# Moving the weights to another DMA queue and re-ranking a planner's tasks in an fp32 threshold-attention and feed-forward kernel

## The chip, the cores and the metric

The kernel runs on one core of a Trainium2 chip. Its metric is the device time of one execution in microseconds (us); lower is better. All times quoted are medians of several executions in the fast state. The span, which the profile uses, runs from the first to the last instruction of one profiled execution and lies 1.7 to 2.2 us under that execution's time. Engines are named as in the profile: PE is TensorE, DVE is VectorE, ACT is ScalarE, POOL is GpSimd, SP is SyncE. A name with a small q behind it ("SPq") is that engine's sequencer issuing DMAs.

## The reference

Attention in which all scores lower than the row's maximum minus tau are dropped, then a feed-forward layer with a sigmoid-weighted activation, all in fp32:

```python
# q, k, v: (8, 8, 576, 64); tau = 0.02; w_in: (512, 2048); w_out: (2048, 512)
scores = scale * np.matmul(q, k.transpose(0, 1, 3, 2))
thresh = np.max(scores, axis=-1, keepdims=True) - tau
scores = np.where(scores >= thresh, scores, -1000000000.0)
scores = scores - np.max(scores, axis=-1, keepdims=True)
attn = np.exp(scores)
attn = attn / (np.sum(attn, axis=-1, keepdims=True) + 1e-09)
x = np.matmul(attn, v)            # then (8, 8, 576, 64) -> (4608, 512)
h = x @ w_in
g = h * (1.0 / (1.0 + np.exp(-1.702 * h)))
out = g @ w_out
```

The two weights arrive as 64-bit floats (they are scaled by 1/np.sqrt of an integer), so the kernel converts 32 pieces of 128 x 512 elements to fp32 itself.

## The kernel before

Two heads make a pair; there are 32 pairs. For each pair the kernel loads q, k and v, transposes q and k on VectorE, multiplies them on TensorE, copies the scores to SBUF on ScalarE, finds each query's maximum on VectorE, subtracts it there, masks and exponentiates on ScalarE, and multiplies with v on TensorE. When the four pairs of a batch item are done, blocks of 512 tokens go through the feed-forward layer, which is most of TensorE's work.

Nothing of the order is left to a compiler. Each piece of work is a `task` with an engine, an estimated cost, a rank, and buffers that it takes and gives back. A small planner simulates the engines and, whenever one is free, emits the ready task of the lowest rank. The rank of a pair's tasks is its number, so the emitted order of each engine follows from ranks and costs; at run time each engine works through its list in order. The early pairs borrow space that the feed-forward layer uses later, so a tile of theirs can be named gT; early weight pieces likewise pass through w_out.

```python
def task(engine, cost, rank, f, *a, after=(), take=(), give=(), lag=0.06):
    tasks.append((engine, cost, rank, f, a, [x for x in after if x is not None],
                  take, give, lag))
    return len(tasks) - 1
...
def load_qk(n, which, queue):              # one of a pair's q or k: 4 transfers
    ...
    for h in range(2):
        for j in range(2):
            queue.dma_start(               # rows of 32 fp32 = 128 bytes
                out=blocks[ds(64 * h + 32 * j, 32), :, :],
                in_=src[b, 2 * hp + h, :, ts(j, 32)].rearrange("(c p) d -> p c d", p=32),
            )
...
def load_w(i):                             # one weight piece, 64-bit: rows of 4 KB
    ...
    nc.sync.dma_start(out=t.rearrange("p c w -> p (c w)"), in_=dram.bitcast(U32))
    nc.sync.dma_start(                     # the same bytes again, shifted by 3
        out=t3.rearrange("p c w -> p (c w)").bitcast(U8)[:, 0 : 8 * WC - 3],
        in_=dram.bitcast(U8)[:, 3 : 8 * WC],
    )
...
def sub(n, t):                             # score * scale - (maximum * scale - tau)
    ...
    nc.vector.scalar_tensor_tensor(
        out=s, in0=s, scalar=scl, in1=mb, op0=ALU.mult, op1=ALU.subtract
    )
...
def exps(n, t):
    nc.scalar.activation(out=s, in_=s, func=AF.Exp, bias=shift)
...
# ranks: weights, and all the tasks of pair n
rank = NPAIR - 0.4 + 0.5 * i / n_in if i < n_in else NPAIR - 0.16 + 0.9 * (i / n_in - 1)
...
r = float(n)                               # loads of q and k: r - 2.0; of v: r - 1.2
```

Two transfers per weight piece, 32 pieces and 512 KB each make 33.5 MB. SyncE issues nearly all transfers of the kernel (ScalarE issues only pair 0's k), so a weight piece stands in one line with q, k and v.

Of the kernel before, what the change touches and what calls it, by code (L numbers as in the profile page):

```python
# [19 lines left out]
P = 128  # L20
GELU_SCALE = 1.702
EPS = 1e-9

# [6 lines left out]
def kernel(  # L30
# [33 lines left out]
    NKT = 4  # L64
# [14 lines left out]
    work = ctx.enter_context(tc.tile_pool(name="work", bufs=2))  # L79
    psA = ctx.enter_context(tc.tile_pool(name="psA", bufs=3, space=bass.MemoryType.PSUM))  # L80
# [6 lines left out]
    kd = [const.tile([P, P], FP32, name=f"kd{i}") for i in range(2)]  # L87
# [4 lines left out]
    tau_b = const.tile([P, 1], FP32, name="tau_b")  # L92
    scl = const.tile([P, 1], FP32, name="scl")
    shift = const.tile([P, 1], FP32, name="shift")
# [6 lines left out]
    limits = {"psA": 3, "psM": 2, "s_m": 7, "s_t": 2, "io": 3, "xT": 3, "mb": 1,  # L101
              "raw0": 1, "raw1": 1, "qkT0": 1, "qkT1": 1, "v_m": 2, "w64": 2}
# [3 lines left out]

    def task(engine, cost, rank, f, *a, after=(), take=(), give=(), lag=0.06):
        tasks.append((engine, cost, rank, f, a, [x for x in after if x is not None],
                      take, give, lag))
        return len(tasks) - 1  # L110

# [117 lines left out]
    def load_w(i):  # L229
        dst, src, c, j = pieces[i]  # L230
        dram = src[ts(c, P), ts(j, WC)]
        if not wide:
            nc.sync.dma_start(out=dst[:, c, ts(j, WC)], in_=dram)
            return


        x = stage(i)
        if x is None:
            t = work.tile([P, WC, 2], U32, name="w64", tag="w64", bufs=2)
            t3 = work.tile([P, WC, 2], U32, name="w64s", tag="w64s", bufs=2)  # L240
        else:
            rows = [w_out[:, ds(PER_STAGE * x + 2 * y, 2), :] for y in range(2)]
            t, t3 = (
                r.rearrange("p a b -> p (a b)").bitcast(U32).rearrange("p (c w) -> p c w", w=2)
                for r in rows
            )
        nc.sync.dma_start(out=t.rearrange("p c w -> p (c w)"), in_=dram.bitcast(U32))
        nc.sync.dma_start(
            out=t3.rearrange("p c w -> p (c w)").bitcast(U8)[:, 0 : 8 * WC - 3],
            in_=dram.bitcast(U8)[:, 3 : 8 * WC],  # L250
        )
        cv[i] = t[:, :, 1], t[:, :, 0], t3[:, :, 0]
# [37 lines left out]
    mats, sT, stats, mbs, pss = {}, {}, {}, {}, {}  # L290
# [7 lines left out]
    def prep_kd(n):  # L298
        for h in range(2):
            nc.scalar.copy(  # L300
                out=kd[n % 2][ts(h, D), ts(h, D)], in_=mats[n, 1][ts(h, D), MAIN:S]
            )
# [4 lines left out]
    def scores(n, t, c):  # L307
        qT, kT = mats[n, 0], mats[n, 1]
        ps = psA.tile([P, 2, 512], FP32, name="ps", tag="ps")
        if t == NKT:  # L310
            for i in range(2):
                nc.tensor.matmul(  # L312
                    ps[:, i, 0:SH], lhsT=kd[n % 2], rhs=qT[:, ts(i, SH)],
                    start=True, stop=True,
                )
            del mats[n, 0], mats[n, 1]
        else:
            for h in range(2):
                nc.tensor.matmul(  # L319
                    ps[:, h, 0:SH],  # L320
                    lhsT=kT[ts(h, D), ts(t, P)], rhs=qT[ts(h, D), ts(c, SH)],
                    start=True, stop=True,
                )
        pss[n, t, c] = ps

    def keep(n, t, c):
# [3 lines left out]
        else:  # L330
            if c == 0:
                st = home(n, "s_m", 2 * S, "s_m", 7, f"s_m{t}")
# [7 lines left out]
    def in_groups(n, t, op):  # L340

        if (n, op) not in stats:
            stats[n, op] = [
                work.tile([P, NKT, 2 * QB], FP32, name="part", tag="part", bufs=2),
                work.tile([P, QB], FP32, name="part_t", tag="part_t", bufs=3),
# [8 lines left out]
    def over_tiles(n, op):  # L354

        pm, pt = stats[n, op]
        r = work.tile([P, 2 * QB], FP32, name="red", tag="red", bufs=3)
# [8 lines left out]
    def over_groups(n, op):  # L366
        r = stats[n, op]
        o = work.tile([64, 2 * QB], FP32, name="fold", tag="fold")
# [4 lines left out]
    def lower(n):  # L373
# [3 lines left out]
            out=f[0:32], in0=stats[n, ALU.max][0:32], scalar1=scl[0:32],  # L377
            scalar2=tau_b[0:32], op0=ALU.mult, op1=ALU.subtract,
# [3 lines left out]
        stats[n, ALU.max] = f  # L382

# [6 lines left out]

    def sub(n, t):
        mb, s = mbs[n], sT[n, t]
        if t < NKT:
            nc.vector.scalar_tensor_tensor(  # L394
                out=s, in0=s, scalar=scl, in1=mb, op0=ALU.mult, op1=ALU.subtract
            )
        else:
            for h in range(2):
                x = s[ts(h, D)]
                nc.vector.scalar_tensor_tensor(  # L400
                    out=x, in0=x, scalar=scl[ts(h, D)], in1=mb[ts(h, D), h, :],
                    op0=ALU.mult, op1=ALU.subtract,
                )
# [5 lines left out]
    def exps(n, t):  # L409
        s = sT[n, t]  # L410
        nc.scalar.activation(out=s, in_=s, func=AF.Exp, bias=shift)  # L411
# [58 lines left out]
    def spread_sums(n):  # L470
# [3 lines left out]
        rc = work.tile([P, S], FP32, name="rc", tag="rc")  # L474
# [63 lines left out]
    nc.sync.dma_start(  # L538
        out=tau_b, in_=bass.AP(tensor=tau.tensor, offset=tau.offset, ap=[[0, P], [1, 1]])
    )  # L540
    for t in kd + v_t + [ones_t]:
        nc.gpsimd.memset(t, 0.0)
    nc.gpsimd.memset(ones, 1.0)
    nc.gpsimd.memset(rebias, -896.0 * 2.0**23)
    for h in range(2):
        nc.gpsimd.memset(ones_t[ts(h, D), h, :], 1.0)

    def tau_terms():



        nc.vector.tensor_scalar(
            out=scl, in0=tau_b, scalar1=0.0, scalar2=SCALE, op0=ALU.is_ge, op1=ALU.mult
# [4 lines left out]
        nc.vector.tensor_single_scalar(out=shift, in_=tau_b, scalar=-1.0, op=ALU.mult)  # L558




    FIRST, LAST = -1.0, 1000.0
    BY_PE = 5
    LEAD = 6

    ready_w = []
    for i in range(len(pieces)):
        rank = NPAIR - 0.4 + 0.5 * i / n_in if i < n_in else NPAIR - 0.16 + 0.9 * (i / n_in - 1)
        if not wide:  # L570
            ready_w.append(task("SP", 0.6, rank, load_w, i, lag=2.5))
# [3 lines left out]
        a = task("SP", 1.1, rank, load_w, i, take=place, lag=5.0)  # L575
        e = task("DVE", 0.44, rank, cv_ex, i, after=[a])
        m = task("ACT", 0.72, rank, cv_power, i, after=[e])
# [3 lines left out]
        ready_w.append(task("DVE", 0.72, rank, cv_end, i, after=[a, m] + over, give=place))  # L581

    tau_done = task("DVE", 1.0, -2.0, tau_terms)
# [5 lines left out]
    def feed_forward(blk):  # L589
        b = -(-(blk + 1) * BLK // S) - 1  # L590
        xs = [placed[n] for n in range(NPAIR * (b + 1))]
        for j in range(NFC):
            for p in range(2):
                after = ffn[-1:] + xs[-NPAIR:]
                if blk == 0:
# [3 lines left out]
                    "PE", 1.79, LAST, mm1, blk, j, p, after=after,  # L599
# [4 lines left out]
                "DVE", 0.7, FIRST, gelu, j, after=[a, last_mm2.get(j // 2)],  # L604
                give=("psM", "io"),
            )
        for i in range(BLK // P):
            for p in range(NFC // 2):
                after = ffn[-1:] + [gelus[2 * p], gelus[2 * p + 1]]
                if blk == 0:  # L610
# [3 lines left out]
                    "PE", 1.79, LAST, mm2, i, p, after=after, take=("psM",) if p == 0 else (),  # L614
# [10 lines left out]
    for n in range(NP):  # L625
        gate = per_pair * (n - LEAD)
        after = ffn[gate : gate + 1] if gate >= 0 else []
        r = float(n)
        q0, q1 = (nc.sync, nc.scalar) if n == 0 else (nc.sync, nc.sync)
# [3 lines left out]
        pq = task("DVE", 0.78, r, prep, n, 0, after=[lq], take=own(n, "qkT0"), give=own(n, "raw0"))  # L633
        pk = task("DVE", 0.78, r, prep, n, 1, after=[lk], take=own(n, "qkT1"), give=own(n, "raw1"))
        pd = task("ACT", 0.5, r, prep_kd, n, after=[pk])
        mx = []
        for t in range(NKT + 1):
            tail = t == NKT
            copies = []
            for c in range(1 if tail else 2):  # L640

                a = task(
                    "PE", 1.1 if tail else 0.58, r, scores, n, t, c,
                    after=[pq, pk] + ([pd] if tail else []) + after,
                    take=("psA", "s_t") if tail else ("psA",) + (own(n, "s_m") if c == 0 else ()),
                    give=own(n, "qkT0", "qkT1") if tail else (),
                )
                after = [a]
                copies.append(task("ACT", 0.64, r, keep, n, t, c, after=[a], give=("psA",)))
            mx.append(task("DVE", 0.78 if tail else 1.37, r, in_groups, n, t, ALU.max, after=copies))  # L650
        a = task("DVE", 0.75, r, over_tiles, n, ALU.max, after=mx)
        a = task("DVE", 0.75, r, over_groups, n, ALU.max, after=[a])
        a = task("DVE", 0.6, r, lower, n, after=[a, tau_done])
        m = task("DVE", 1.38, r, spread_max, n, after=[a], take=own(n, "mb"))
        ws, subs = [], [m]
        for t in range(NKT + 1):
            tail = t == NKT
            a = task(
                "DVE", 1.5 if tail else 1.37, r, sub, n, t, after=subs[-1:],
                give=own(n, "mb") if tail else (),  # L660
            )
            subs.append(a)
            a = task("ACT", 0.7 if tail else 1.17, r, mask, n, t, after=[a])
            ws.append(task("ACT", 0.88 if tail else 1.36, r, exps, n, t, after=[a]))
        back = own(n, "s_m") * NKT + ("s_t",)
        every = range(NKT + 1)
        if n < NPAIR:

            pv = den = None
            for t in every:  # L670
                first = t == 0
                den = task(
                    "PE", 1.1, r, sums_by_pe, n, [t], True, after=[ws[t], den],
# [3 lines left out]
                    "PE", 1.1, r, values, n, [t], after=[ws[t], den, pv, lv],  # L677
                    take=("psA",) if first else (), give=(back[t],) if t < NKT else ("s_t", "v_m"),
                )
            a = task("DVE", 1.2, r, one_row, n, after=[den], give=("psM", "psM"))  # L680
        else:
            pv = task("PE", 5.0, r, values, n, every, after=ws + [lv], take=("psA",), give=("v_m",))
        if NPAIR <= n < BY_PE:
            a = task("PE", 5.2, r, sums_by_pe, n, every, False, after=ws + [pv], take=("psA",), give=back)
            a = task("DVE", 1.2, r, one_row, n, after=[a], give=("psA",))
        elif n >= BY_PE:
            su = [
                task("DVE", 0.78 if t == NKT else 1.37, r, in_groups, n, t, ALU.add, after=[ws[t]])
                for t in range(NKT + 1)
            ]  # L690
            a = task("DVE", 0.75, r, over_tiles, n, ALU.add, after=su + [pv], give=back)
            a = task("DVE", 0.75, r, over_groups, n, ALU.add, after=[a])
            a = task("DVE", 0.7, r, one_group, n, after=[a])
        a = task("DVE", 1.05, r, spread_sums, n, after=[a])
        b, hp = divmod(n, NPAIR)
        new = {(b * S + x) // BLK for x in cuts(b)[:-1]} if hp == 0 else set()
        if b:
            new -= {(b * S - 1) // BLK}
        placed[n] = task(
            "DVE", 0.9, r, place_x, n, after=[a, pv], take=("xT",) * len(new), give=("psA",)  # L700
# [35 lines left out]
```

## Time and profile before

| | before |
|---|---|
| time, median of 4 | 1448.2 us (1447.3 to 1449.3) |
| span | 1446.5 us |
| TensorE busy / idle | 1384.0 / 62.5 us |
| first matmul | 7.95 us |
| pair 5's last subtraction ends | 219.2 us |
| pair 5's values start on TensorE | 226.66 us |

Three more views matter for what follows. The first is SyncE's queue in the timeline before: start, duration, line, what is loaded. The first two lines are the issues of pair 1's q and k (the early pairs borrow space that the feed-forward layer uses later, so the tile is named gT; early weight pieces likewise pass through w_out):

```profile
6.64 2.20 SPq L189 DMA_DIRECT2D gT<-in_q_dram  x4
8.89 2.12 SPq L189 DMA_DIRECT2D gT<-in_k_dram  x4
...
29.12 5.58 SPq L189 DMA_DIRECT2D gT<-in_q_dram  x4
34.80 4.99 SPq L189 DMA_DIRECT2D gT<-in_k_dram  x4
```

Four issues take 2.1 to 2.2 us. The duration is that of the issuing, not of the transfer: the page gives a median of 2.3 us from issue to landing for each single one of q_raw's transfers. The last two lines are pair 3's q and k, which stand directly behind the first weights in the same queue: there the issuing takes 5.58 and 4.99 us, but VectorE does not wait for them. The second view is the busy time of each engine in two stretches, before and after 40 us, up to 330 us, from where TensorE is full (from 330 to 1420 us it is busy for 1089.95 to 1090.00 of 1090 us in the six kernels of this study that were asked for it):

```profile
0.00:40.00 40.00, 22.32 (x132) 13.14 (x132) 28.91 (x47) 22.13 (x32) 1.34 (x13) 0.87 0.84 228
40.00:330.00 290.00, 248.94 (x1037) 119.26 (x1035) 260.20 (x434) 164.02 (x219) 0.00 (x0) 0.92 0.40 120
```

The columns are the stretch, its length, then busy us (and instructions) of PE, PE's weight loads, DVE, ACT and POOL, then the granted clock, the DMA engines' share and GB/s. VectorE's third pair of numbers is the one to follow: 28.9 us of work in the first 40, and 289.1 us in the first 330. The third view is the page's rows of the subtraction and the exponential (busy, mean ns of one, idle before):

```profile
L394 DVE SCALAR_TENSOR_TENSOR s_m<-s_m,scl,mb 128x1152 f32<-128x1152 f32 x120 | 163.3, 1411 | 0.6
...
L411 ACT ACTIVATE s_m<-s_m,shift 128x1152 f32<-128x1152 f32 x120 | 150.2, 1252 | 2.5
```

### The profile page before, as it was taken

The page shows a single profiled execution, that of the slowest core. Times are in us where ns is not written, and L with a number is a line of the kernel's source. Part 1 is how long each engine was busy: PE and PEld are TensorE (multiplying, and loading weights), DVE is VectorE, ACT ScalarE, POOL GpSimd, SP SyncE. Part 2 cuts the span into 40 slices and gives each one's busy share as a digit, 9 for nine tenths or more (in the row PEclk, how much of TensorE's full clock was granted, in tenths as well). Part 3 has the DMA queues.
Part 4 walks back from the last instruction along what each step waited for, and adds up shares of the span by engine and source line. Part 5 has one row for each costly group of instructions (what it writes and reads, how often), then busy time and mean ns, then how long its engine had stood idle before and what let it go on. Part 6 is the DMA issues. An engine that isn't in the chain of part 4 may idle for free.

```text
span 1446.5 us, 13628 instructions
## 1 busy us (share of the span) xinstructions
PE 1384.0 (96%) x4936; PEld 650.1 (45%) x4936; DVE 997.7 (69%) x1650; ACT 643.6 (44%) x885; POOL 1.3 (0%) x13
## 2 busy tenths in 40 slices
PE   5769979899999999999999999999999999999998
PEld 3334434344444444444444444444444444444443
DVE  7998998888978888888878886788777820200100
ACT  5675544555545554555555554455445500100100
POOL 0000000000000000000000000000000000000000
PEclk8879999999999999999999999999999999999999
DMA  8239461111122012211111111111110000000000
GB/s 240 49 130 287 146 251 40 40 25 25 27 44 49 15 29 39 47 32 25 25 40 39 25 25 39 40 25 21 32 36 16 1 7 22 0 7 22 0 7 22
DMA packets 205074, 72.18 MB, mean 50 GB/s; under 512 B 192208, under 2 KB 192208, under 8 KB 205008
## 3 DMA queue, kind: packets, MB, share of 16 engines
q1 hardware_dynamic: 202640, 71.03, 19.1%
q8 instruction: 39, 0.64, 0.2%
q10 hardware_dynamic: 2368, 0.30, 0.1%
q14 instruction: 27, 0.22, 0.1%
HBM read 61.85 MB, written 9.44 MB: 49 GB/s over the span
## 4 chain that ended last, share of the span: by engine, by line
PE 88%; DVE 8%; ACT 1%; DMA 1%; issue 1%; DVEq 0%; ACTq 0%; SPq 0%
PE ops L523 33%; PE hps L504 31%; PE pv L425 11%; PE ps L319 9%; PE ps L312 2%; PE den L425 2%; DVE part L352 1%; DVE s_m L394 1%; DMA w64s<-in_moe_w_out_dram 1%; DVE mb L386 1%; DVE gT L515 0%; DVE w_out L284 0%; DVE w64s L276 0%; DVE part_t L352 0%; ACT s_m L338 0%
## 5 line engine op out<-in xcount | busy, mean ns | idle before, releaser
L523 PE MATMUL ops<-w_out,gT 128*128 128x512 f32 x1152 | 507.0, 597 | 7.4 <-DVE w_out L284 7.3
L504 PE MATMUL hps<-xT,w_in 128*128 128x512 f32 x1152 | 507.6, 596 | 1.5 <-DVE gT L515 1.4
L352 DVE TRANSPOSE_TENSOR_REDUCE part<-s_m 128x36 f32<-128x1152 f32 x228 | 301.3, 1355 | 107.4 <-ACT s_m L338 106.5
L523 PEld LDWEIGHTS ops<-w_out,gT 128*128 128x128 f32 x1152 | 217.7, 191 | 278.6 <-issue 265.7
L504 PEld LDWEIGHTS hps<-xT,w_in 128*128 128x128 f32 x1152 | 215.3, 190 | 274.2 <-issue 244.4
L515 DVE SCALAR_TENSOR_TENSOR gT<-th,hps 128x512 f32<-128x512 f32 x144 | 97.2, 675 | 226.4 <-ACT th L512 225.8
L338 ACT COPY s_m<-ps 128x576 f32<-128x576 f32 x240 | 137.2, 657 | 144.5 <-PE ps L319 143.3
L407 ACT ACTIVATE s_m<-s_m 128x1152 f32<-128x1152 f32 x120 | 138.4, 1153 | 119.7 <-DVE s_m L394 119.6
L512 ACT ACTIVATE th<-hps 128x512 f32<-128x512 f32 x144 | 85.3, 592 | 229.6 <-PE hps L504 229.5
L394 DVE SCALAR_TENSOR_TENSOR s_m<-s_m,scl,mb 128x1152 f32<-128x1152 f32 x120 | 163.3, 1411 | 0.6
L319 PE MATMUL ps<-qkT 64*128 64x288 f32 x960 | 141.8, 433 | 17.3 <-DVE qkT L295 17.3
L411 ACT ACTIVATE s_m<-s_m,shift 128x1152 f32<-128x1152 f32 x120 | 150.2, 1252 | 2.5
L425 PE MATMUL pv<-s_m,v_m 128*64 128x288 f32 x960 | 126.2, 414 | 0.0
L319 PEld LDWEIGHTS ps<-qkT 64*128 64x128 f32 x960 | 83.2, 190 | 89.4 <-issue 40.4
L530 ACT ACTIVATE osb<-ops 128x512 f32<-128x512 f32 x36 | 21.3, 591 | 220.4 <-PE ops L523 220.4
L425 PEld LDWEIGHTS pv<-s_m,v_m 128*64 128x64 f32 x960 | 67.5, 139 | 64.2 <-issue 15.0
L400 DVE SCALAR_TENSOR_TENSOR s_t<-s_t,scl,mb 64x576 f32<-64x576 f32 x60 | 48.7, 812 | 0.4
L492 DVE TENSOR_TENSOR xT<-pv,rc 128x288 f32<-128x288 f32 (+8 forms) x96 | 28.4, 351 | 22.4 <-PE pv L425 21.1
L352 DVE TRANSPOSE_TENSOR_REDUCE part_t<-s_t 128x18 f32<-128x576 f32 x59 | 43.7, 741 | 0.0
L386 DVE STREAM_TRANSPOSE mb<-thr 128x1152 f32<-128x1152 f32 x30 | 41.3, 1377 | 0.9
L312 PE MATMUL ps<-qkT,kd 128*128 128x288 f32 x120 | 37.1, 432 | 0.0
L425 PE MATMUL pv<-s_t,v_t 128*64 128x288 f32 x256 | 36.5, 406 | 0.0
(66 smaller groups left out, 571.1 us busy)
## 6 DMA issues: line engine op xcount, KB each, us to landing
out_dram<-osb SPq DMA_DIRECT2D x36, 256.0 KB, 2.0
q_raw<-in_q_dram SPq DMA_DIRECT2D x120, 72.0 KB, 2.3
k_raw<-in_k_dram SPq DMA_DIRECT2D x116, 72.0 KB, 2.3
v_m<-in_v_dram SPq DMA_DIRECT2D x64, 128.0 KB, 2.4
w_out<-in_moe_w_in_dram SPq DMA_DIRECT2D x12, 512.0 KB, 6.5
w<-in_moe_w_out_dram SPq DMA_DIRECT2D x12, 512.0 KB, 5.0
w_out<-in_moe_w_in_dram SPq DMA_DIRECT2D x12, 511.6 KB, 7.4
w64s<-in_moe_w_out_dram SPq DMA_DIRECT2D x12, 511.6 KB, 6.0
```

The lines of the kernel that those rows point to most:

```text
L312: nc.tensor.matmul(ps[:, i, 0:SH], lhsT=kd[n % 2], rhs=qT[:, ts(i, SH)], start=True, stop=True,)
L319: nc.tensor.matmul(ps[:, h, 0:SH], lhsT=kT[ts(h, D), ts(t, P)], rhs=qT[ts(h, D), ts(c, SH)], start=True, stop=True,)
L338: nc.scalar.copy(out=o, in_=pss.pop((n, t, c))[:, :, 0:SH])
L352: nc.vector.tensor_reduce(out=o, in_=i, axis=AXL.X, op=op, apply_transpose=True)
L394: nc.vector.scalar_tensor_tensor(out=s, in0=s, scalar=scl, in1=mb, op0=ALU.mult, op1=ALU.subtract)
L407: nc.scalar.activation(out=s, in_=s, func=AF.Prelu, alpha=STEEP)
L411: nc.scalar.activation(out=s, in_=s, func=AF.Exp, bias=shift)
L425: nc.tensor.matmul(o[c][ts(h, D), 0:SH], lhsT=lhsT, rhs=rhs, start=(t == 0), stop=(t == NKT),)
L504: nc.tensor.matmul(hidden[j], lhsT=w_in[:, c, ts(j, P)], rhs=xTs[blk][:, c, :], start=(c == 0), stop=(c == NDC - 1),)
L512: nc.scalar.activation(out=ths[j], in_=hidden[j], func=AF.Tanh, scale=GELU_SCALE / 2)
L515: nc.vector.scalar_tensor_tensor(out=gT[j], in0=ths.pop(j), scalar=1.0, in1=hidden.pop(j), op0=ALU.add, op1=ALU.mult)
L523: nc.tensor.matmul(acc[i], lhsT=gT[j][:, ts(i, P)], rhs=w_out[:, j, :], start=(j == 0), stop=(j == NFC - 1),)
```

## The change

The change has these parts, each with its intent.

- *Ranks by kind of task.* A rank is shifted by a number that depends on the function, with one table for the first eight pairs and one for the rest; the weights' ranks and the planner's estimated costs are set anew.
- *Weights from POOL's queue*, so that SyncE's queue has q, k and v alone. tau is loaded from there too.
- *Plain subtraction.* The scale moves from the subtraction into the exponential, where ScalarE multiplies by a per-partition number.
- *Eight score buffers* where there were seven, paid for by single buffers elsewhere.
- A table load moved ahead of the first scores, and a path that spreads the maxima by DMA, which `BY_DMA = 0` leaves unused.

```diff
-    limits = {... "s_m": 7, ...
+    limits = {... "s_m": 8, ...
+    EARLY = {"lower": -1.16, "values": 0.42, "exps": 0.63, "load_qk": -1.86,
+             "prep": -1.45, "sums_by_pe": 1.44, "one_row": 1.22, "mask": 0.52}
+    LATER = {"in_groups": 1.11, "values": 1.2, "one_group": 1.46, "prep": -1.37}
     def task(engine, cost, rank, f, *a, after=(), take=(), give=(), lag=0.06):
+        if 0 <= rank < LAST:
+            rank += (EARLY if a[0] < 2 * NPAIR else LATER).get(f.__name__, 0.0)
 ...
-        nc.sync.dma_start(out=t.rearrange("p c w -> p (c w)"), in_=dram.bitcast(U32))
-        nc.sync.dma_start(
+        nc.gpsimd.dma_start(out=t.rearrange("p c w -> p (c w)"), in_=dram.bitcast(U32))
+        nc.gpsimd.dma_start(
 ...
-            nc.vector.scalar_tensor_tensor(
-                out=s, in0=s, scalar=scl, in1=mb, op0=ALU.mult, op1=ALU.subtract
-            )
+            nc.vector.tensor_tensor(out=s, in0=s, in1=mb, op=ALU.subtract)
 ...
-        nc.scalar.activation(out=s, in_=s, func=AF.Exp, bias=shift)
+        nc.scalar.activation(out=s, in_=s, func=AF.Exp, scale=scl, bias=shift)
 ...
-        rank = NPAIR - 0.4 + 0.5 * i / n_in if i < n_in else NPAIR - 0.16 + 0.9 * (i / n_in - 1)
+        rank = 3.71 + 0.45 * i / n_in if i < n_in else 4.19 + 0.07 * (i / n_in - 1)
-        a = task("SP", 1.1, rank, load_w, i, take=place, lag=5.0)
-        e = task("DVE", 0.44, rank, cv_ex, i, after=[a])
+        a = task("POOL", 2.4, rank, load_w, i, take=place, lag=5.0)
+        e = task("DVE", 0.43, rank + 0.22, cv_ex, i, after=[a])
 ...
+    warm = task("ACT", 1.5, -2.0, first_act)
 (cut: tau's terms, thresholds on unscaled scores, costs of other tasks, unused DMA path)
```

## The prediction

Passages of the prediction and of two expectations are cut, because they rested on figures or mechanisms that no trace of this case had shown. The sums in it stand as they were recorded, and one of their terms is among the cuts: what the cheaper subtraction takes off VectorE's work ahead of the mark, put at -2.0 us. The sum of -3.6 us is thus +1.5 - 3.1 - 2.0, and 215.6, 219.1, 1438.1 and 1436 contain the term. (The rows measured afterwards give 24 x 59 ns + 12 x 62 ns = 2.2 us for it.) Also cut are the forecast lengths of the subtraction and the exponential, rival 3 (weights from POOL's queue are late in themselves) and rival 4 (VectorE's time after 325 us counts after all); where the prediction names rival 3 further down, it means that.

> **What bounds the kernel now.** I read the page's busy shares and slices first, then TensorE's and VectorE's timelines for the first 362 us with their waits, then the chain of waits of that stretch, then the DMA slices of the first 40 us.
>
> ```profile
> PE 1384.0 (96%) x4936; PEld 650.1 (45%) x4936; DVE 997.7 (69%) x1650; ACT 643.6 (44%) x885; POOL 1.3 (0%) x13
> ...
> PE   5769979899999999999999999999999999999998
> ...
> DVE  7998998888978888888878886788777820200100
> ...
> PEclk8879999999999999999999999999999999999999
> ```
>
> The reader is to see two regimes. From slice 10 on (about 325 us) PE is full at full clock: nothing that VectorE, ScalarE or a DMA saves there moves the end. Before it PE has gaps and a lower granted clock, while DVE is at 80 to 100%. All that can be won is the 62.5 us in which PE is idle (1446.5 - 1384.0). These are its large waits:
>
> ```profile
> 7.95 6.58 PE L319 MATMUL ps<-qkT 64*128 64x288 f32 x32 [7.95 <-DVE qkT L295]
> 25.43 2.19 PE L425 MATMUL den<-s_m,ones 128*64 128x288 f32 x8 [9.72 <-ACT s_m L411]
> 54.62 2.19 PE L425 MATMUL den<-gT,ones 128*64 128x288 f32 x8 [4.02 <-ACT gT L411]
> 74.64 2.19 PE L425 MATMUL den<-s_m,ones 128*64 128x288 f32 x8 [7.16 <-ACT s_m L411]
> 103.05 2.19 PE L425 MATMUL den<-gT,ones 128*64 128x288 f32 x8 [10.49 <-ACT gT L411]
> 216.36 10.30 PE L523 MATMUL ops<-w_out,gT 128*128 128x512 f32 x18 [6.28 <-DVE w_out L284]
> 292.55 2.29 PE L319 MATMUL ps<-qkT 64*128 64x288 f32 x8 [9.39 <-DVE qkT L295]
> ```
>
> They sum to 55 us; the tail after the last matmul is 3.8 us (the window from 1400 us on has 42.74 us of PE in 46.5). Up to 225 us they are all one thing: PE has no work until VectorE has finished a pair's maximum, subtraction and division, or a weight's conversion. VectorE itself idles little: 3.5, 2.4 and 3.1 us before its first reduction at 11.01 us, then about 6 us in small waits up to 219 us. So filling PE's early gaps wins nothing by itself; the kernel gets earlier only if VectorE gets through its early work earlier, or if PE stands in front of a wait with something else to do. The wait at 292.55 is of the second kind: a pair's scores stand ahead of the previous pair's values in PE's order, and the transposes they need stand late in VectorE's.
>
> The DMA engines' first 40 us, one digit per microsecond:
>
> ```profile
> DMA  0059993488887648889798999999999999999428
> ```
>
> They are busy with q, k and v up to about 19 us, and with the first six megabytes of weights from 18 to 37 us. There is no free room at the start.
>
> [...] Nothing in the trace before has two loaded queues at once, so how they share is not shown yet. [...] the scalar_tensor_tensor it replaces shows 1411 and 812 ns here. [...] the exponential, with a bias pointer alone, shows 1252 ns[...].
>
> **The change part by part.** The built program's order (which has no times in it) gives the counts below.
>
> *Subtraction.* [...] Ahead of pair 5's last subtraction are 24 full and 12 half ones[...].
>
> *Ranks.* I take pair 5's last subtraction as the mark. In both orders VectorE has ahead of it six pairs' maxima and subtractions, all 32 weight conversions and all 16 GELUs. So the new order cannot remove VectorE's early work, only shuffle it. The differences: two more transposes (2 x 0.74 = +1.5), pair 4's division not yet done (two reductions, reciprocal, transpose, multiplication: 0.97 + 0.2 + 0.27 + 0.78 + 0.9 = -3.1)[...]. Sum -3.6 us. The mark before is the end of this row, at 219.2 us:
>
> ```profile
> 217.56 1.64 DVE L400 SCALAR_TENSOR_TENSOR s_t<-s_t,scl,mb 64x576 f32<-64x576 f32 x2
> ```
>
> So it comes at 215.6 us plus the change d in VectorE's idle time. ScalarE then needs about 3.5 us (in part a full mask and exponential, then the half ones, 0.67 and 0.78 in the trace), so PE can start pair 5's values at 219.1 + d. Before it started at 226.66, held by the wait of 6.28 us on w_out. That wait goes: only six of the second layer's tasks (four matmul records each) stand ahead of pair 5's values, where there were twelve.
>
> *PE from there on.* Before: 1446.5 - 226.66 = 1219.8 us, less the wait of 9.39, about 0.5 of small ones and the tail of 3.8: 1206.1 us of work. The new order has six second-layer tasks more to do (6 x 1.72 = +10.3; 24.03 us for 56 records is 1.72 for four) and pair 6's scores already done (-5.6: 32 records at 3.35/24 plus 1.17). The wait of 9.39 goes as well: pair 8's transposes now stand ahead of pair 7's last subtraction. But PE's order is cut up more: 75 stretches of feed-forward matmuls after the second block begins, where there were 62. What a cut costs:
>
> ```profile
> 305.01 24.03 PE hps L504 x56
> ...
> 334.05 1.17 PE ps L319 x8
> 335.22 1.91 PE hps L504 x4
> ...
> 340.22 2.18 PE ps L319 x16
> ```
>
> Four records alone take 1.91 against 1.72, and scores of 8 + 8 take 2.34 against 2.18 for 16: some 0.3 us a cut, 13 x 0.3 = +3.9. Sum 1206.1 + 10.3 - 5.6 + 3.9 + 3.8 + 0.5 = 1219.0 us.
>
> *Score buffers.* Eight instead of seven let two whole pairs of the ordinary kind be in flight. The waits on copies (18 us of VectorE's idle time in the first 362) are mostly after 230 us, where PE decides; I count nothing.
>
> *Start.* The table load (1.28 us at 7.98 in the trace) moves ahead of the first scores, but k's issue on ScalarE's queue now stands behind it, and tau comes by POOL: about even.
>
> *Weights from POOL.* SyncE no longer stands behind them; the two waits on w64s landings (0.55 and 1.39) may go. But they are issued from about 3 us, on top of q, k and v.
>
> So the span is 219.1 + 1219.0 + d = 1438.1 + d. For d: of VectorE's 6 us of small waits about 5 should go, as the divisions now stand behind other work (2.7 us waiting for den) and weights come early (2); against that I put +2 for the start. d = -3, span 1435; the unprofiled time is 1.4 us above the span, so 1436.
>
> **The rivals.**
> 1. *The weights collide with q and k.* Pair 1's k is now seventh of the loads on SyncE's queue, behind pair 2's, and its transpose stands in VectorE's order before pair 0's maximum is folded. Alone these seven loads occupy the DMA engines until about 17 us; shared half and half with weights from 4 us on, k would land at about 4 + 2 x (15 - 2) = 25 to 30 us. VectorE would stand 6 to 10 us, and all else moves by as much: 1441 to 1447. For it: the digits above. Against it: small packets may get more than half.
> 2. *The order fits well and nothing stalls.* The planner's costs were corrected; PE then starts pair 5's values when the last GELUs allow, not before about 213 us, and the cuts cost nothing: some 1424. Against more than this: VectorE's list ahead of the mark is the same.
> 3. [...]
> 4. [...]
>
> **Range and chances.** The mark moves one for one with d, which I put between -12 and +10; the cuts are uncertain by 3. That gives 1422 to 1449. Faster by over 2% (below 1419.5) would need VectorE to lose under 2 us after its first data: 0.06. Slower by over 2% needs rivals 1 and 3 far beyond their estimates: 0.03.
>
> **What would show it.** Right: PE full from pair 5's values, at 214 to 222 us; no wait of 6.28 nor of 9.39; VectorE's first 200 us as full as before[...]. Wrong: a gap of VectorE on gT from k before 30 us (rival 1), repeated waits on w64s (rival 3), or PE gaps after 325 us. If pair 5's values start before 210 us, my claim that VectorE's early work fixes the time is wrong.

## The result, and the profile after

The kernel after took 1451.9 us (median of 4, 1449.2 to 1452.6), against 1448.2. The ratio is 1.0022, with a 95% interval from 1.0005 to 1.0039. Ratios here are the mean time of one kernel's fast runs over that of the other's of the same rounds, so they are not quite the ratio of the medians. Both kernels are correct. The change made the kernel a little slower, by less than 2%, where 1436 with a range of 1422 to 1449 had been predicted.

The page's slices after, one digit per 36 us:

```profile
PE   2687899999999999999999999999999999999998
...
DVE  3999989989989889767867886787867720200100
```

From the sixth slice on every digit of TensorE but the last is 9, where before that began at the ninth. But the first two digits are 2 and 6 where there were 5 and 7, and VectorE's first digit is 3 where it was 7. The gain and the loss are both in this line. TensorE's large waits after, in time order (start, duration, what, in brackets the idle time and what ended it; left out are nine waits of 1.4 to 6.6 us from 44 to 167 us):

```profile
10.49 6.65 PE L344 MATMUL ps<-qkT 64*128 64x288 f32 x32 [10.49 <-DVE qkT L320]
34.27 6.66 PE L344 MATMUL ps<-gT 64*128 64x288 f32 x32 [15.96 <-DVE gT L320]
...
308.13 3.32 PE L344 MATMUL ps<-qkT 64*128 64x288 f32 x24 [1.01 <-DVE xT L543]
```

The waits of 6.28 us on w_out and of 9.39 us on a transpose are gone, and past 172 us there is nothing over the 1.01 shown. In their place stands a wait of 15.96 us for pair 1's transposes, before TensorE has done any pair's values. VectorE's timeline tells what its transposes waited for:

```profile
26.89 0.78 DVE L320 STREAM_TRANSPOSE gT<-gT 128x576 f32<-128x576 f32 x1 [12.01 <-DMA gT<-in_q_dram]
...
33.35 0.78 DVE L320 STREAM_TRANSPOSE gT<-gT 128x576 f32<-128x576 f32 x1 [1.25 <-DMA gT<-in_k_dram]
```

VectorE stands 12.01 us in front of pair 1's q, because the transpose is next in its list: the three maxima behind it, whose scores ScalarE had copied by 17.97 us, run at 27.59, as soon as the transpose is done. SyncE's queue shows why q is late:

```profile
6.30 15.92 SPq L214 DMA_DIRECT2D gT<-in_q_dram  x4
22.32 4.76 SPq L214 DMA_DIRECT2D q_raw<-in_q_dram  x4
27.19 2.06 SPq L214 DMA_DIRECT2D k_raw<-in_k_dram  x4
29.29 2.12 SPq L214 DMA_DIRECT2D gT<-in_k_dram  x4
```

The same four issues that took 2.20 us before take 15.92 us. What is beside them is in the DMA slices of the first 40 us after, one digit and one rate per microsecond:

```profile
DMA  0099999999999999999999998378888888756683
GB/s 0 18 194 181 136 195 319 287 281 369 402 422 394 391 402 392 395 371 386 405 397 392 354 214 110 60 120 130 136 138 132 140 137 137 133 131 145 108 132 58
```

Before, the loads of q, k and v ran at 80 to 160 GB/s from 6 to 18 us, and the weights came after that. Now the first six weight pieces (6.3 MB) start at 2.46 us and the engines move 350 to 420 GB/s from 9 to 23 us. In these 14 us SyncE issues only pair 1's q (0.3 MB), so nearly everything that moves is weights. SyncE's issues are back at 2.1 us from 27 us on, when the six pieces are in (the last one, issued at 14.01 us, lands some 11 us later).

The cost over the whole early part is seen in the stretches up to 330 us, after:

```profile
0.00:40.00 40.00, 13.55 (x62) 9.69 (x64) 15.50 (x29) 11.63 (x21) 8.26 (x26) 0.79 0.89 231
40.00:330.00 290.00, 257.05 (x1117) 124.16 (x1114) 267.54 (x453) 181.47 (x239) 28.47 (x52) 0.94 0.44 123
```

VectorE did 15.5 us of work in the first 40 where it had done 28.9, which is 13.4 us lost; from there to 330 us it did 267.5 where it had done 260.2, which is 7.3 us won. What became of the subtraction and the exponential is in the page's rows after:

```profile
L462 ACT ACTIVATE s_m<-s_m,shift,scl 128x1152 f32<-128x1152 f32 x120 | 160.4, 1343 | 2.6
...
L447 DVE TENSOR_TENSOR s_m<-s_m,mb 128x1152 f32<-128x1152 f32 x120 | 156.6, 1352 | 0.8
```

The subtraction takes 1352 ns where it took 1411; the exponential 1343 where it took 1252, so 91 ns more with the scale as a second per-partition operand.

### The profile page after: what moved, and what is told of

Read it like the earlier page. It is cut to its first block, busy times and chain, and to the rows that moved or that the text cites. A ratio compares the mean times of both kernels' runs of the same rounds, so it can differ in the third digit from the quotient of the medians.

```text
span 1450.8 us, 13674 instructions
## 1 busy us (share of the span) xinstructions
PE 1387.5 (96%) x4936; PEld 651.0 (45%) x4936; DVE 986.6 (68%) x1653; ACT 659.9 (45%) x886; POOL 36.7 (3%) x78
## 3 DMA queue, kind: packets, MB, share of 16 engines
q10 hardware_dynamic: 2368, 0.30, 0.2%
## 4 chain that ended last, share of the span: by engine, by line
PE 88%; DVE 7%; ACT 2%; SPq 2%; issue 1%; DMA 0%; DVEq 0%; ACTq 0%
PE hps L555 34%; PE ops L574 34%; PE pv L476 9%; PE ps L344 9%; PE ps L337 2%; SPq L214 2%; DVE part L377 1%; ACT s_m L458 1%; DVE gT L447 1%; ACT s_m L462 1%; DVE w_in L309 1%; DVE w_out L301 0%; PE den L476 0%; DVE s_t L452 0%; DVE qkT L320 0%
## 5 line engine op out<-in xcount | busy, mean ns | idle before, releaser
L555 PEld LDWEIGHTS hps<-xT,w_in 128*128 128x128 f32 x1152 | 215.6, 190 | 269.7 <-issue 253.6
L462 ACT ACTIVATE s_m<-s_m,shift,scl 128x1152 f32<-128x1152 f32 x120 | 160.4, 1343 | 2.6
L344 PE MATMUL ps<-qkT 64*128 64x288 f32 x960 | 146.0, 438 | 14.4 <-DVE qkT L320 12.8
L447 DVE TENSOR_TENSOR s_m<-s_m,mb 128x1152 f32<-128x1152 f32 x120 | 156.6, 1352 | 0.8
L581 ACT ACTIVATE osb<-ops 128x512 f32<-128x512 f32 x36 | 21.4, 594 | 285.3 <-PE ops L574 285.3
L452 DVE TENSOR_TENSOR s_t<-s_t,mb 64x576 f32<-64x576 f32 x60 | 45.0, 750 | 0.4
```

What stands on the lines that cost most here:

```text
L344: nc.tensor.matmul(ps[:, h, 0:SH], lhsT=kT[ts(h, D), ts(t, P)], rhs=qT[ts(h, D), ts(c, SH)], start=True, stop=True,)
L447: nc.vector.tensor_tensor(out=s, in0=s, in1=mb, op=ALU.subtract)
L462: nc.scalar.activation(out=s, in_=s, func=AF.Exp, scale=scl, bias=shift)
L555: nc.tensor.matmul(hidden[j], lhsT=w_in[:, c, ts(j, P)], rhs=xTs[blk][:, c, :], start=(c == 0), stop=(c == NDC - 1),)
```

## The experiments

My theory after reading the traces: the change consists of a win of some 12 us from the order, and a loss of some 15 us from weights that are issued too early on a second queue. The rivals: (a) POOL's queue is slow in itself; (b) the new order is what puts VectorE in front of late data, and the queue matters little; (c) the win comes from the eighth buffer or from the subtraction.

The experiments ran in three groups, each on one chip with its own runs of the kernel before: 1447.9 us (7 runs), 1447.5 (9) and 1447.7 (7). All outputs are right.

### The old kernel with its weights on POOL's queue

```diff
-        nc.sync.dma_start(out=t.rearrange("p c w -> p (c w)"), in_=dram.bitcast(U32))
-        nc.sync.dma_start(
+        nc.gpsimd.dma_start(out=t.rearrange("p c w -> p (c w)"), in_=dram.bitcast(U32))
+        nc.gpsimd.dma_start(
```

The planner's costs and ranks are untouched, so TensorE, VectorE and ScalarE have exactly the order of before (the built programs agree instruction by instruction on these three engines).

> The kernel before with one thing changed: the 64 weight transfers are issued from POOL's queue instead of SyncE's, everything else in the same order on PE, VectorE and ScalarE. Theory (the weights collide with q and k at the start): the first six megabytes run from about 3 us, pair 1's q and k land some 10 us late, and the time becomes 1453 to 1464 us. Rival (the collision is harmless by itself, the new order made it costly): 1446 to 1450. [...]

Measured: 1461.4 us (4 runs), ratio 1.0088 (1.0073 to 1.0103). SyncE's queue:

```profile
1.19 2.96 SPq L189 DMA_DIRECT2D q_raw<-in_q_dram  x4
...
5.40 5.36 SPq L203 DMA_DIRECT2D v_t<-in_v_dram  x1
10.80 1.66 SPq L199 DMA_DIRECT2D v_m<-in_v_dram  x1
12.50 6.13 SPq L203 DMA_DIRECT2D v_t<-in_v_dram  x1
18.67 5.81 SPq L189 DMA_DIRECT2D gT<-in_q_dram  x4
```

and VectorE's first transpose:

```profile
21.39 0.78 DVE L295 STREAM_TRANSPOSE qkT<-q_raw 128x576 f32<-128x576 f32 x1 [17.37 <-DMA q_raw<-in_q_dram]
```

A single issue of a small v tail stretched from about 0.5 to 5.4 and 6.1 us. Even pair 0's q, whose transpose starts at 6.46 us in the kernel before, arrived at 21.4. Its issues had ended at 4.15 us, as early as before (4.21), so it is the transfers themselves that were held up, and not only their issuing. TensorE's first matmul moved from 7.95 to 22.89 us, and the wait on w_out came at 228.66 us in place of 216.36, still 6.28 us long. So the delay of the start, 14.9 us, is carried nearly whole to the end (13.2 us of span). Rival (b) falls: the queue alone does it, in the old order. There are no repeated waits on later weight pieces.

### The new kernel with its weights back on SyncE's queue

```diff
-        nc.gpsimd.dma_start(out=t.rearrange("p c w -> p (c w)"), in_=dram.bitcast(U32))
-        nc.gpsimd.dma_start(
+        nc.sync.dma_start(out=t.rearrange("p c w -> p (c w)"), in_=dram.bitcast(U32))
+        nc.sync.dma_start(
 ...
-        a = task("POOL", 2.4, rank, load_w, i, take=place, lag=5.0)
+        a = task("SP", 1.1, rank, load_w, i, take=place, lag=5.0)
```

> The changed kernel with the weight transfers back on SyncE's queue, ranked anew by the planner with the old issue cost of 1.1. Theory: VectorE's wait of 12 us on pair 1's q goes, 10 to 15 us come back, 1436 to 1442 us. Rival (the order is at fault): 1448 to 1453. SyncE standing behind weights again may cost some us of that.

Measured: 1436.3 us (4 runs), ratio 0.9913 (0.9898 to 0.9928). SyncE's issue of pair 1's q is back at its old length:

```profile
5.45 2.20 SPq L214 DMA_DIRECT2D gT<-in_q_dram  x4
```

The first weight issue comes at 20.90 us, behind the q and k of the early pairs. TensorE's first two waits are 8.48 us (against 10.49) and 2.87 us (against 15.96). The stretches of this kernel:

```profile
0.00:40.00 40.00, 25.14 (x134) 15.76 (x136) 29.39 (x50) 24.15 (x36) 1.86 (x14) 0.87 0.94 234
40.00:330.00 290.00, 262.67 (x1133) 125.79 (x1130) 267.32 (x463) 173.91 (x234) 0.00 (x0) 0.95 0.43 123
```

VectorE has its 29.4 us in the first 40 again and keeps its 267.3 after that. By 330 us it has done 13.7 us more than in the kernel after (296.7 against 283.0), and the time is 15.6 us shorter. The new order without the early weights beats the kernel before by 11.6 us. The kernel after was timed in another group, but the two groups' kernels before differ by 0.3 us only. The planner, which sees the weights on another engine, also orders some work anew: the built programs of this run and of the kernel after differ in the operation at 166 of VectorE's 1653 places and at 62 of TensorE's 2468. So this run alone does not separate queue and order. The waits account for the difference without the order, though: VectorE's 12.01 and 1.25 us for q and k are gone, and TensorE starts 2.01 us earlier, together 15.3 of the 15.6 us.

### The new kernel, POOL's queue, weights held until pair 1's k has landed

Before its first weight, POOL copies one column of a landed tile, so that its queue waits there; the planner has the same condition.

```diff
+    HOLD = (1, 1)                      # pair 1, k
 ...
+        if i == 0:
+            nc.gpsimd.tensor_copy(out=hold, in_=landed[HOLD][:, 0:1])
 ...
+        if n == HOLD[0]:
+            for w in weights:
+                tasks[w][5].append(lk)
```

> The changed kernel, weights still from POOL's queue, but POOL first copies one column of pair 1's k, so that its first weight transfer waits until that k has landed. PE's order is the same up to the first feed-forward matmul. Theory: the waits on pair 1's q and k go, pair 1's scores start before 20 us instead of at 34.3, the time is 1435 to 1441 us. Rival (order[...]): 1446 to 1452.

Measured: 1442.1 us (4 runs), ratio 0.9957 (0.9942 to 0.9972): only part of the loss came back, and the time is a microsecond over the range expected. The collision had moved on to the next load in SyncE's queue, pair 3's k:

```profile
19.31 13.20 SPq L217 DMA_DIRECT2D gT<-in_k_dram  x4
```

VectorE waits 5.73 us for it, until 41.40 us (5.7 us are also what is missing to the 1436.3 of SyncE's queue), and TensorE's wait ahead of its matmuls at 55.01 grew to 12.60 us. That a part of the cure gave a part of the gain (9.9 of 15.6 us) speaks for the theory, and the place where the rest went names the remedy: hold the weights until the last early load is in.

### The same, held until pair 3's k has landed

```diff
-    HOLD = (1, 1)
+    HOLD = (3, 1)
```

> The changed kernel with POOL held until pair 3's k has landed, instead of pair 1's. In the run held to pair 1's k, pair 3's k took 13.2 us to issue beside the weights, and PE waited 12.6 us at 55 us. Theory: the collision was only moved there; now no q or k of the first four pairs is hit, and the time is that of weights on SyncE, 1434 to 1439 us. Rival (POOL's queue is slower in itself): stays at 1440 to 1444.

Measured: 1435.4 us (5 runs), ratio 0.992 (0.9908 to 0.9933). POOL's copy runs at 23.61 us and the weights are issued from 24.08:

```profile
23.61 0.49 POOL L267 COPY hold<-gT 128x1 f32<-128x1 f32 x1 [21.15 <-DMA gT<-in_k_dram]
```

TensorE's first two waits are 8.53 and 2.69 us, and the one between 40 and 60 us is 6.75, where it was 12.60. The built programs of the two held runs have the same operations in the same order on every engine; only the tile that POOL waits for differs, so what lies between them (6.7 us by the medians, 5.4 by the ratios, of two groups) comes from the moment at which the weights start. Against the kernel after, TensorE's and SyncE's orders are the same and VectorE's differs at 52 of 1653 places. POOL's queue is thus as good as SyncE's (1436.3 in the other group) once it starts late enough, and rival (a) falls: it is when the weights are issued, not who issues them.

### A second hardware queue in place of POOL's

The kernel before, with the first six weight pieces issued by ScalarE directly behind pair 0's k, and the rest by SyncE as ever. TensorE's and VectorE's orders are those of before.

```diff
+        queue = nc.scalar if i < 6 else nc.sync
-        nc.sync.dma_start(out=t.rearrange("p c w -> p (c w)"), in_=dram.bitcast(U32))
-        nc.sync.dma_start(
+        queue.dma_start(out=t.rearrange("p c w -> p (c w)"), in_=dram.bitcast(U32))
+        queue.dma_start(
 (cut: in the planner the six tasks move to ScalarE, behind pair 0's k)
```

> The kernel before, with its first six weight pieces (twelve transfers) issued from ScalarE's queue, directly behind pair 0's k, instead of from SyncE's queue at about 18 us; the order on TensorE and VectorE is the one before. Theory A, the wide rows of any second queue take the DMA engines from q's and k's short rows: SyncE's issues between 3 and 20 us are stretched as in the run with POOL's queue (5 to 6 us for pair 1's q or a v tail, against 2.2 and 0.5 before), the DMA slices are full from 4 to 17 us, TensorE's first matmul comes after 12 us, and the time is 1453 to 1462. Theory B, it is POOL's software queue that does it: SyncE's issues keep their 2.2 and 0.5 us and pair 0's transposes their time; ScalarE reaches its table load about 2 us late because it issues twelve transfers at some 0.5 us each, TensorE starts its first tail late by as much, and the time is 1446 to 1451.

Measured: 1463.1 us (4 runs), ratio 1.0107 (1.0091 to 1.0124). SyncE's queue:

```profile
6.71 5.44 SPq L189 DMA_DIRECT2D gT<-in_q_dram  x4
12.65 13.05 SPq L189 DMA_DIRECT2D gT<-in_k_dram  x4
```

The stretching is there with a hardware queue as well (the page calls POOL's queue software_dynamic, ScalarE's and SyncE's hardware_dynamic), so it is not a property of POOL's software queue. Of theory A's marks, the stretched issues of q and the full DMA slices held; the v tails kept their 0.5 us, the first matmul at 9.55 us (over 12 was said) did not come so late, and the time is a microsecond over its range. The time itself cannot be put down to SyncE's loads alone here: ScalarE's own weight issues were held up too, and it reached its table load at 22.37 us where it had been 7.98, so TensorE's next matmuls waited 12.08 us for its copies. This run shows that loads beside weights from ScalarE's queue are held up too (13.05 us for k's four issues), not what that costs.

### The new kernel on SyncE's queue, without the rank offsets

```diff
-    EARLY = {"lower": -1.16, ...}
-    LATER = {"in_groups": 1.11, ...}
+    EARLY, LATER = {}, {}
 ...
-        rank = 3.71 + 0.45 * i / n_in if i < n_in else 4.19 + 0.07 * (i / n_in - 1)
+        rank = NPAIR - 0.4 + 0.5 * i / n_in if i < n_in else NPAIR - 0.16 + 0.9 * (i / n_in - 1)
 (the weights' +0.22 and -0.47 removed too)
```

> The changed kernel with weights on SyncE, but all ranks as they were before: no offsets by kind of task, and the weights' old ranks. If the offsets by kind make the gain: back to 1444 to 1450 us, with the waits of about 6 us on w_out and about 9 us on the transposes back. Rival (buffers and subtraction make it): 1434 to 1440.

Measured: 1450.5 us (5 runs), ratio 1.002 (1.0008 to 1.0033), half a microsecond over the range expected. All that the order had won is gone, and a little more: some 13 to 15 us against the three kernels of the same group that have the offsets (1435.4 to 1437.2). In TensorE's timeline the waits of the kernel before are back:

```profile
25.76 2.19 PE L466 MATMUL den<-s_m,ones 128*64 128x288 f32 x8 [9.70 <-ACT s_m L452]
...
217.27 11.65 PE L564 MATMUL ops<-w_out,gT 128*128 128x512 f32 x22 [6.49 <-DVE w_out L299]
...
287.13 2.19 PE L466 MATMUL pv<-s_m,v_m 128*64 128x288 f32 x8 [3.25 <-ACT s_m L452]
```

I had expected a wait of some 9 us on transposes near 290 as well; there were only 3.25 us and several of under 1. VectorE's work up to 330 us is 284.4 us, against 296.7 with the offsets. Part of it, 4.40 us at 129 us and 1.57 behind that, is spent waiting for weight pieces to land. So the ranks are the win: the offsets and the weights' ranks together, which no run separated.

### Seven buffers, and the subtraction alone

Seven score buffers in the new kernel on SyncE's queue:

```diff
-    limits = {... "s_m": 8, ...
+    limits = {... "s_m": 7, ...
-                st = home(n, "s_m", 2 * S, "s_m", 8, f"s_m{t}")
+                st = home(n, "s_m", 2 * S, "s_m", 7, f"s_m{t}")
```

> The changed kernel with weights on SyncE (1436 us) and seven score buffers instead of eight. My estimate: the eighth buffer is worth little, 1435 to 1440 us. Rival (it is what lets VectorE run through the first pairs): 1443 or more.

Measured: 1437.2 us (5 runs), ratio 0.9929 (0.9917 to 0.9942). Against eight buffers (1436.3 us in another group, and 1436.2 in this group with the small changes of the last experiment below), the eighth buffer is worth about a microsecond.

The subtraction, thresholds and exponential of the change in the kernel before, with the terms of tau that they need, and nothing else (cut to the two main places):

```diff
-            nc.vector.scalar_tensor_tensor(
-                out=s, in0=s, scalar=scl, in1=mb, op0=ALU.mult, op1=ALU.subtract
-            )
+            nc.vector.tensor_tensor(out=s, in0=s, in1=mb, op=ALU.subtract)
 ...
-        nc.scalar.activation(out=s, in_=s, func=AF.Exp, bias=shift)
+        nc.scalar.activation(out=s, in_=s, func=AF.Exp, scale=scl, bias=shift)
```

> The kernel before with the plain subtraction alone (the scale goes into the exponential). My estimate: 2 us less VectorE work before 219 us, so 1445 to 1449 us; the subtraction shows near 1352 ns and the exponential near 1343. If the subtraction mattered more, under 1442.

Measured: 1446.7 us (4 runs), ratio 0.9986 (0.9969 to 1.0002): a microsecond or nothing, as expected. Rival (c) falls with these two and with the run before them, which has both the eighth buffer and the plain subtraction, and wins nothing.

### Trying for more at the start

The new kernel on SyncE's queue, with ScalarE issuing pair 0's k ahead of its table load and tau's small terms behind pair 0's transposes in VectorE's order:

```diff
-    tau_done = task("DVE", 1.0, -2.0, tau_terms, after=[warm])
+    tau_done = task("DVE", 1.0, -0.5, tau_terms, after=[warm])
 ...
+            tasks[warm][5].append(lk)
 ...
+            tasks[tau_done][5].extend([pq, pk])
```

> The changed kernel with weights on SyncE, k's issue again ahead of ScalarE's table load, and tau's terms on VectorE behind pair 0's transposes. Theory: VectorE's first wait of 6.1 us on tau goes, pair 0's scores start at about 7 us instead of 8.48, and everything follows: 1433 to 1436 us, 1 to 2 us under the version with weights on SyncE alone.

Measured: 1436.2 us (5 runs), ratio 0.992 (0.9907 to 0.9934): no gain that could be told from none. VectorE no longer waits for tau, but then waits for q until 6.66 us, and the first matmul comes at 8.15 us in place of 8.48. The step that I had taken for the bound of the start had q right behind it. None of the three versions near 1436 us can be told from the others; each beats both the kernel before and the kernel after by some 0.8% or more.

## Why the prediction was wrong

The sum was "219.1 + 1219.0 + d" with d = -3; taken from the trace, it is 234.06 + 1216.7. The term that failed is d, "the change d in VectorE's idle time", of which the prediction said "against that I put +2 for the start. d = -3". The mark, pair 5's last subtraction, ends here in the kernel after:

```profile
228.23 1.51 DVE L452 TENSOR_TENSOR s_t<-s_t,mb 64x576 f32<-64x576 f32 x2
```

That is 229.74 us, so d = 229.74 - 215.6 = +14.1, not -3: 17 us off, and the time is 16 us off. With the weights back on SyncE's queue the mark ends at 213.82, so d = -1.8, and the time is the 1436 that was predicted. The one step that went wrong is therefore the start, and in it the early weights.

- *The mechanism was rival 1, too small and not chosen.* "The weights collide with q and k" named the place and the sign. It said "shared half and half", pair 1's k as the load that would hang, a stand of VectorE of "6 to 10 us", and a time of 1441 to 1447. Measured: pair 1's q hangs first, VectorE stands 12.01 us for it and 1.25 more for k, and the total is 15.6 us against the kernel without the collision. The wrong size is the sharing. q got far less than half of the bytes; that the loads would merely run at half speed was an assumption which no line of the trace before could support, as the text said itself (two queues are at work there only for pair 0's q and k, whose rows are alike). Measured, q was 0.3 of the some 6 MB that moved from 6.3 to 22.2 us. A warning did stand in the trace before, unused: q's and k's issues behind the weights on one queue, 5.58 and 4.99 us long. Its one reserve, "small packets may get more than half", pointed the wrong way, and it drew the upper end of d at +10. The range was also narrower than its parts: 1438.1 + 10 for d, 3 for the cuts and 1.4 for the unprofiled time make 1452.5 at the upper end, and 1424.5 at the lower, where 1449 and 1422 were given. (The 1.4 is 1.8 in the execution profiled after.)
- *"Start: about even" was wrong, by about half a microsecond at the least.* tau from POOL's queue landed at 6.12 us in the run with the weights on SyncE, against 3.47 to 3.5 from SyncE's own queue, and TensorE's first matmul came at 8.48 us against 7.95; the collision made it 10.49.
- *"VectorE's early work fixes the time" held.* A delay of VectorE in the first 40 us reached the end nearly whole: against the kernel on SyncE's queue, 13.9 us of its work were lost by 40 us and 15.6 us of time at the end. The strongest case is the old kernel on POOL's queue, with 14.9 us at the start and 13.2 at the end.
- *The removed waits were right.* The 6.28 us and the 9.39 us went, and TensorE is full from 172 us on but for 1.01 us. "PE from there on" was 1219.0 us and measured 1450.8 - 234.06 = 1216.7; the cuts cost no more than was put for them.
- *The small parts were right.* The subtraction, put at 2.0 us in the sum, gave 1.2 by itself, within its interval of nothing; the buffers were put at 0 and are worth about 1; that weights from POOL's queue are late in themselves (rival 3) was not seen: with all 64 transfers on POOL's queue and the collision taken away the time was 1435.4 us, against 1436.3 on SyncE's queue.
- *One thing stays half explained.* Pair 5's values in the run on SyncE's queue start at 220.83 us, 7 us behind the mark and without a wait, where "219.1 + d" would give 217.3: TensorE itself had become the bound there by some 3.5 us. It made up for it behind, 1434.2 - 220.83 = 1213.4 against 1219.0. So that 1436 came out is in part two errors that cancel.

How the DMA engines share is shown only from outside: four issues of q took 15.92 us beside weights from POOL's queue, and four of k 13.05 us beside weights from ScalarE's, against 2.20 and 2.12 us before. Nor is a second queue needed for long issues, as the 5.58 us before show; what hurt was weights under way while a load that is needed next is issued. The trace after also tells what moved: in the first 40 us POOL's queue carried its 6.29 MB in 1376 packets, while pair 0's k, a load of the same shape as pair 1's q, took 2368 packets for 0.30 MB. So q was a small part of the bytes, though not of the packets, and it came in only with the last of the weights: its issue ended at 22.2 us and VectorE's wait for it at 26.89, and the weights' rates end at about 23. By what rule the engines share was not shown; no run changed the length of rows or packets.

## What to carry to other kernels

A load that is moved to an empty queue no longer starts where it used to stand (the first weight issue came at 2.46 us here, where it had been 17.77); ask what it will then run beside, and if those are loads that an engine waits for next, hold the moved load until they have landed: here the new kernel took 1451.9 us with the weights at once and 1435.4 with the weights held. The length of an issue is not fixed: four issues of pair 1's q took 2.20 us in the kernel before and 15.92 beside weights from POOL's queue, and four of pair 3's q took 5.58 behind weights on the same queue. Where several parts of a change come to nothing together, run each alone: here a gain of 12 us and a loss of 15 were hidden in a difference of 4. An engine that works through its list in order stands where its next input is late (VectorE 12.01 us for pair 1's q), so a re-ranking and a change of queue must be judged together.
